# A zero fill by DMA: rows copied as they are, or rows cast from bf16 to f32

## The chip, the core and the metric

The kernel runs on one core of a Trainium2 chip. The metric is the device time of one execution in microseconds (us); the time before is the median of three runs, 823.16 us (822.59 to 823.45). One further view, a profile, records every instruction and every DMA transfer of one execution. In its pages PE is the matmul engine (PEld its weight loads), DVE the vector engine, ACT the scalar engine, POOL the engine that issues the zero fill, and SP the engine that issues most other DMAs. All DMAs, whoever issues them, are carried by the same 16 DMA engines.

## The reference

One decoder layer at decode time, forward and backward. Two sequences (B = 2) with one token each pass through layer norm, attention over a cached window, a residual, layer norm, a gated GELU network and a residual. Only the last 4,096 of 32,768 cached keys and values take part:

```python
W = min(4096, max(256, Sk // 4))              # Sk = 32768, so W = 4096
k = jnp.repeat(k_cache[:, :, Sk - W:, :], rep, axis=1)
v = jnp.repeat(v_cache[:, :, Sk - W:, :], rep, axis=1)
p = softmax(q @ k * Dh**-0.5);  o = p @ v
h = x + o @ wo;   h2 = h + B(layernorm(h))    # B: (gelu(x@wg) * (x@wu)) @ wd
```

The outputs are h2 and the gradients by the input, both caches and all weights. The gradient of each cache is as large as the cache (2 x 8 x 32768 x 128 in bf16, 134 MB), and its first 28,672 positions of every (sequence, head) are zero, because the window does not reach them. So the kernel must write 32 regions of 28,672 x 128 bf16 zeros, 7.34 MB each, 234.9 MB together.

## The kernel before

**The zero fill.** Line 99 makes a tile `zt` of 128 partitions x `ZE` bf16 elements, with `ZE` = 2048 (line 98), so 4 KiB in each partition. Line 122 fills it with zeros on DVE, by an AND with 0 of the first loaded weights (so it waits for the load of wq). Lines 186 and 187 call `zero_cast` once for each of the 32 regions; each call issues one DMA from POOL (line 104). The region is seen as 128 partitions x `nper` = 14 rows x 2048 elements, and the tile is repeated 14 times as the source, so a DMA consists of 1,792 rows of 4 KiB, and the whole fill of 57,344 rows. Source and destination are both bf16: nothing is converted. POOL issues the first eight DMAs in one go and each later one when an earlier one has landed.

**The rest of the work** runs beside the fill, in this order: layer norm and q; `attention(0)`, the loop over the eight key/value heads of sequence 0 (lines 309 to 446); `middle(0)`, output projection and feed-forward network forward and backward; `score_grads(0)`; then `attention(1)` and `middle(1)`; `score_grads(1)` with the weight gradients filled in; the gradients of wq (lines 717 to 754); and last the gradients of the caches' windows (lines 756 to 790), stored in 32 DMAs of 1 MB from SP (line 788). Keys, values and weights are loaded by SP (lines 116 to 145), each as soon as its place in SBUF is free.

**One large SBUF tile**, `mem`, holds nearly everything at hand-set offsets (lines 35 to 63); a place is reused when its last reader is done. The loop `m_unit` (lines 374 to 395) makes products of keys and exponentials in small buffers `pK` for the matmuls of line 394. It works on `pk_j` key columns at a time:

```python
for (n, h0, h1) in ((pk_j, 0, 2), (pk_j - 1, 2, 3)):
    ...  # DVE, line 380: two instructions a unit
for (jj, i) in [(jj, 3) for jj in range(pk_j)] + [(pk_j - 1, 2)]:
    ...  # ACT, line 383: pk_j + 1 instructions a unit
```

For sequence 0 `pk_j` is 4 and there are three buffers of 4 KiB; for sequence 1 it is 2, with three buffers of 2 KiB (lines 53 to 55). In both cases 32 columns of a head make up its `n_u` = 32 / `pk_j` units.

The end of the program waits, on SP, for all DMAs that write outputs, the zero fill's among them (it shows in the waits as line 813).

Of the kernel before, what the change touches and what calls it, by code (L numbers as in the profile page):

```python
# [8 lines left out]
F32 = mybir.dt.float32  # L9
# [7 lines left out]
P = 128  # L17
B, D = 2, 512
HQ, HKV, REP, DH = 32, 8, 4, 128
# [13 lines left out]
KIB = 1024  # L33

OFF_V = 0
OFF_M = 64 * KIB
# [3 lines left out]
OFF_WU = 150 * KIB  # L40
OFF_WD = 164 * KIB
OFF_R = 178 * KIB
OFF_KT = 186 * KIB
OFF_E = (190 * KIB, 192 * KIB)
OFF_DS = (194 * KIB, OFF_M)
MEM_BYTES = 196 * KIB
OFF_R0, OFF_R1, OFF_R2 = OFF_R, OFF_R + 2 * KIB, OFF_R + 4 * KIB
OFF_LN2B, OFF_XR = OFF_R + 6 * KIB, OFF_R + 7 * KIB
OFF_X, OFF_X_AGAIN = OFF_LN2B, OFF_M + 2 * KIB

K_OFF = ([OFF_WG + (g % 4) * 8 * KIB for g in range(HKV)],
         [OFF_WD, OFF_WD + 8 * KIB, 32 * KIB, 40 * KIB, 48 * KIB, 56 * KIB, OFF_WD, OFF_WD + 8 * KIB])
PK_J = (4, 2)
PK_OFF = ([OFF_WG + 32 * KIB + i * 4 * KIB for i in range(3)],
          [OFF_WD + 16 * KIB + i * 2 * KIB for i in range(3)])

OFF_BD = OFF_WO
OFF_GST = OFF_WG
# [7 lines left out]
def kernel(ctx, tc, A_x, A_k_cache, A_v_cache, A_wq, A_wo, B_x, B_w_gate, B_w_up, B_w_down, grad_out,  # L66
                out_0, out_1, out_2, out_3, out_4, out_5, out_6, out_7, out_8):
    nc = tc.nc
    Sk = A_k_cache.shape[2]
    Z = Sk - W  # L70
# [3 lines left out]
    mem_pool = ctx.enter_context(tc.tile_pool(name="mem", bufs=1))  # L74
    mem = mem_pool.tile([P, MEM_BYTES], U8)

    def at(off, shape, dt, name):
        n = int(np.prod(shape[1:])) * mybir.dt.size(dt)
        assert off + n <= MEM_BYTES, (name, off, n)
        ap = mem[0:shape[0], off:off + n].bitcast(dt)  # L80
        dims = " ".join(f"a{i}" for i in range(1, len(shape)))
        return ap.rearrange(f"p ({dims}) -> p {dims}", **{f"a{i}": shape[i] for i in range(1, len(shape))}) if len(shape) > 2 else ap
# [3 lines left out]
    def evac(out, in_):  # L86
        if evac_i[0] % 2 == 0:
            nc.vector.tensor_copy(out=out, in_=in_)  # L88
        else:
            nc.scalar.copy(out=out, in_=in_)  # L90
        evac_i[0] += 1
# [3 lines left out]
    dKv = out_2[:, :, Z:, :].rearrange("b g (p j) d -> p b g j d", p=P)  # L95
    dVv = out_3[:, :, Z:, :].rearrange("b g (p j) d -> p b g j d", p=P)

    ZE = 2048
    zt = const.tile([P, ZE], BF16)
    zero_regions = [o[b, g, 0:Z, :].rearrange("r d -> (r d)") for o in (out_2, out_3) for b in range(B) for g in range(HKV)]  # L100

    def zero_cast(i):
        nper = (Z * DH) // (P * ZE)
        nc.gpsimd.dma_start(out=zero_regions[i].rearrange("(p k e) -> p k e", p=P, k=nper),  # L104
                            in_=zt[:].unsqueeze(1).to_broadcast([P, nper, ZE]))

    dh2_x = at(OFF_XR, [66, D], BF16, "xr")
# [2 lines left out]
    def load_rows(eng):  # L110
        eng.dma_start(out=dh2_bf, in_=grad_out.rearrange("b s d -> (b s) d"))
        eng.dma_start(out=x_32, in_=A_x.rearrange("b s d -> (b s) d"))

    def load_x(off):
# [6 lines left out]
    load_rows(nc.scalar)  # L121
    nc.vector.tensor_scalar(out=zt[:].bitcast(U32), in0=wq_sb[:, 0, 0:ZE].bitcast(U32), scalar1=0, scalar2=None,
                            op0=ALU.bitwise_and)
# [62 lines left out]
    for i in range(len(zero_regions)):  # L186
        zero_cast(i)
# [40 lines left out]
    def tblock(ps_pool, src_block):  # L228
        ps = ps_pool.tile([P, 4, P], BF16, tag="ps_tb", name="ps_tb")
        for a in range(4):  # L230
            nc.tensor.transpose(out=ps[:, a, :], in_=src_block(a), identity=ident_bf[:])  # L231
        dst = at(OFF_KT + (tb_i[0] % 3) * KIB, [P, 4, P], BF16, "tb")
        tb_i[0] += 1
# [40 lines left out]
    M_sb = at(OFF_M, [P, HQ, DH], BF16, "M")  # L274
    E = [at(OFF_E[b], [P, 8, 4, HQ], BF16, f"e{b}") for b in range(B)]
    p_bf = [at(OFF_E[b], [P, 8 * P], BF16, f"p{b}") for b in range(B)]
    ds_bf = [at(OFF_DS[b], [P, 8 * P], BF16, f"ds{b}") for b in range(B)]

# [30 lines left out]
    def attention(b):  # L309
        with tc.tile_pool(name="ps_KT", bufs=2, space=PSUM) as ps_KT, \  # L310
# [16 lines left out]
            S_ps, Ef = {}, {}  # L327
            lsum = small.tile([P, 4, HQ], F32, name="lsum", tag="l4")
            eT = E[b]
            pk_j = PK_J[b]  # L330
            n_pk = len(PK_OFF[b])
            n_u = NJ // pk_j
            kt_every = n_u // 8
# [1 line left out]
            def kt_unit(g, u):  # L335
                KT_ps = ps_KT.tile([P, 8, P], BF16, tag="kt", name="KT_ps")
                for jj in range(8):
                    nc.tensor.transpose(out=KT_ps[:, jj, :], in_=Kt[b, g][:, u * 8 + jj, :], identity=ident_bf[:])  # L338
                KT = at(OFF_KT + (u % 2) * 2 * KIB, [P, 8, P], BF16, "KT")
                evac(KT[:], KT_ps[:])  # L340
# [119 lines left out]
    def middle(b):  # L460
        h0 = b * HQ
        with tc.tile_pool(name="ps_W", bufs=2, space=PSUM) as ps_W, \
# [80 lines left out]
            if b == 1:  # L543
                ffn_ps = ps_B.tile([B, D], F32)
                for k in range(NFR):
                    nc.tensor.matmul(out=ffn_ps[:], lhsT=actT_bf[:, k, :], rhs=wd[:, k, :], start=(k == 0), stop=(k == NFR - 1))
                h2_bf = at(OFF_KT + 3 * KIB, [B, D], BF16, "h2")
                nc.vector.tensor_tensor(out=h2_bf[:], in0=h_sb[:], in1=ffn_ps[:], op=ALU.add)
# [38 lines left out]
    def score_grads(b, filler=None):  # L587
# [4 lines left out]
        with tc.tile_pool(name="ps_S", bufs=1, space=PSUM) as ps_S, \  # L592
# [4 lines left out]
            def produce(i):  # L597
                g, a = units[i]
                VT_ps = ps_T.tile([P, 8, P], BF16, tag="t", name="VT_ps")
                for jj in range(8):  # L600
                    nc.tensor.transpose(out=VT_ps[:, jj, :], in_=Vt[b, g][:, a * 8 + jj, :], identity=ident_bf[:])  # L601
                VT = at(OFF_KT + (i % 2) * 2 * KIB, [P, 8, P], BF16, "VT")
                evac(VT[:], VT_ps[:])
# [18 lines left out]
    ln1_bf = at(OFF_R0, [B, D], BF16, "ln1b")  # L622
    mv1, rstd1 = layernorm(x_bf[:], "1", ln1, ln1_bf)
    attention(0)
    middle(0)
    score_grads(0)
    attention(1)
    middle(1)
    x_bf = load_x(OFF_X_AGAIN)
# [188 lines left out]
```

## Time and profile before

| | |
|---|---|
| median of three runs | 823.16 us (822.59 to 823.45) |
| the profiled execution | 823.45 us |
| its span in the profile | 821.7 us |
| PE / DVE / ACT / POOL busy | 596.9 / 513.5 / 457.4 / 36.3 us |
| moved by DMA | 332.50 MB, mean 405 GB/s |
| HBM read / written | 49.30 MB / 282.33 MB |
| the zero fill: DMAs, MB | 32 of 7.34 MB, issued from 14.5 to 574.3 us |
| last matmul phase ends, last store issued | about 750 us, 755.3 us |

The span is cut into 40 slices of about 20.5 us; in the rows with one digit for each slice, a 9 means 90% or more of the slice. The row DMA is the mean busy share of the 16 DMA engines. In the part on DMA queues, q0 (software) carries what POOL issues, which is the zero fill, and q1 (hardware) what SP issues; the three numbers are packets, megabytes, and the time of the packets as a share of 16 engines' span. A row of 4 KiB is one packet.

### The profile page before, as it was taken

How to read it: one execution, taken by the hardware profiler on the slowest of the kernel's cores; microseconds unless marked ns; L12 is line 12 of the kernel's file. 1: busy time of each engine (PE TensorE's matmuls, PEld its weight loads, DVE VectorE, ACT ScalarE, POOL GpSimd, SP SyncE). 2: the span in 40 equal slices, each digit the busy share in tenths (PEclk: the TensorE clock that was granted, in tenths of full speed). 3: DMA queues.
4: the chain of work that ended last, by engine and by line, in shares of the span. 5: the costliest groups of instructions: out<-in, count | busy, mean ns of one | idle time of the engine just before them, and what ended most of it. 6: DMA issues, size and time to landing. Idle time of an engine off the chain costs nothing.

```text
span 821.7 us, 13560 instructions
## 1 busy us (share of the span) xinstructions
PE 596.9 (73%) x5350; PEld 318.8 (39%) x5350; DVE 513.5 (62%) x1021; ACT 457.4 (56%) x1080; POOL 36.3 (4%) x51
## 2 busy tenths in 40 slices
PE   3788878789788588888857878988595777674000
PEld 3455443275766444444323457443241222221000
DVE  2799999433433499999961255667636899984000
ACT  1899999233334399999870333656443676674000
POOL 4100000000100000000000000000000000000000
PEclk9899999959579799999996775987586888897555
DMA  8999999999999999999999999999999999999995
GB/s 355 422 440 408 420 417 402 417 413 418 405 391 418 421 414 412 411 411 410 410 387 420 415 404 399 408 407 407 408 406 406 407 413 412 414 414 411 415 407 213
DMA packets 69472, 332.50 MB, mean 405 GB/s; under 512 B 1808, under 2 KB 1824, under 8 KB 59296
## 3 DMA queue, kind: packets, MB, share of 16 engines
q0 software_dynamic: 57856, 234.88, 71.3%
q1 hardware_dynamic: 11540, 96.75, 28.6%
q8 instruction: 42, 0.69, 0.3%
q14 instruction: 22, 0.18, 0.1%
q10 hardware_dynamic: 12, 0.01, 0.0%
HBM read 49.30 MB, written 282.33 MB: 404 GB/s over the span
## 4 chain that ended last, share of the span: by engine, by line
PE 41%; ACT 19%; DVE 17%; DMA 11%; issue 3%; SPq 0%; ACTq 0%; DVEq 0%
ACT mem L383 9%; ACT mem L90 9%; DVE mem L380 7%; PE ps_tb L231 7%; PE M_ps L394 6%; DMA out_dram<-mem 6%; DVE mem L88 4%; PE ps_g L780 3%; PE VT_ps L601 3%; PE dP_ps L610 3%; PE ps_gr L671 3%; PE KT_ps L338 2%; PE d_ln_ps L539 2%; PE gu_ps L487 2%; PE oPK_ps L388 2%
## 5 line engine op out<-in xcount | busy, mean ns | idle before, releaser
L380 DVE TENSOR_TENSOR mem<-mem,ef 128x128 bf16<-128x128 bf16 (+3 forms) x384 | 218.1, 615 | 9.3 <-PE M_ps L394 7.6
L383 ACT ACTIVATE mem<-mem,ef 128x128 bf16<-128x128 bf16 x704 | 214.6, 395 | 9.9 <-PE M_ps L394 9.3
L394 PE MATMUL M_ps<-mem 128*128 128x512 bf16 x512 | 155.9, 385 | 28.7 <-DVE mem L380 21.4
L780 PE MATMUL ps_g<-mem 128*128 128x512 bf16 x256 | 82.2, 424 | 26.7 <-ACT mem L90 25.5
L90 ACT COPY mem<-ps_tb 128x512 bf16<-128x512 bf16 x83 | 48.7, 586 | 94.4 <-PE ps_tb L231 72.4
L90 ACT CAST mem<-ps_g 128x512 bf16<-128x512 f32 x128 | 74.7, 586 | 34.5 <-DVE mem L88 30.2
L88 DVE CAST mem<-ps_g 128x512 bf16<-128x512 f32 x128 | 82.4, 687 | 11.9 <-PE ps_g L780 10.6
L231 PE MATMUL ps_tb<-ident_bf,mem 128*128 128x128 bf16 x664 | 80.5, 262 | 8.0 <-DVE mem L88 2.6
L88 DVE COPY mem<-ps_tb 128x512 bf16<-128x512 bf16 x83 | 35.2, 424 | 71.2 <-PE ps_tb L231 43.8
L394 PEld LDWEIGHTS <-mem 128*128 128x128 bf16 x512 | 43.9, 98 | 82.0 <-DVE mem L380 43.2
L231 PEld LDWEIGHTS <-mem 128*128 128x128 bf16 x664 | 54.6, 127 | 34.8 <-issue 26.5
L780 PEld LDWEIGHTS <-mem 128*128 128x128 bf16 x256 | 26.8, 105 | 81.3 <-issue 67.9
L104 POOL DMA_DIRECT2D out_dram<-zt x32 | 33.6, 1133 | 538.0 <-DMA out_dram<-zt 527.3
L338 PE MATMUL KT_ps<-ident_bf,mem 128*128 128x128 bf16 x512 | 49.6, 235 | 10.5 <-DMA mem<-in_A_k_cache_dram 4.6
L90 ACT COPY mem<-VT_ps 128x1024 bf16<-128x1024 bf16 x33 | 33.7, 1022 | 35.8 <-PE VT_ps L601 30.1
L610 PE MATMUL dP_ps<-mem 128*128 128x512 bf16 x128 | 43.1, 413 | 4.5 <-ACT mem L90 4.5
L601 PE MATMUL VT_ps<-ident_bf,mem 128*128 128x128 bf16 x512 | 44.4, 234 | 0.9 <-DVE pkT L577 0.9
L338 PEld LDWEIGHTS <-mem 128*128 128x128 bf16 x512 | 35.9, 105 | 23.6 <-issue 7.2
L601 PEld LDWEIGHTS <-mem 128*128 128x128 bf16 x512 | 36.1, 106 | 21.3 <-issue 13.3
L90 ACT COPY mem<-KT_ps 128x1024 bf16<-128x1024 bf16 x32 | 32.0, 1001 | 19.2 <-PE KT_ps L338 19.2
L671 PE MATMUL ps_gr<-mem 2*128 2x512 bf16 (+1 forms) x78 | 31.1, 471 | 13.4 <-DVE mem L691 7.2
L88 DVE COPY mem<-VT_ps 128x1024 bf16<-128x1024 bf16 x31 | 21.4, 690 | 29.1 <-PE VT_ps L601 28.5
(250 smaller groups left out, 646.6 us busy)
## 6 DMA issues: line engine op xcount, KB each, us to landing
out_dram<-zt POOLq DMA_DIRECT2D x32, 7168.0 KB, 174.6
out_dram<-mem SPq DMA_DIRECT2D x36, 1024.0 KB, 21.3
mem<-in_A_k_cache_dram SPq DMA_DIRECT2D x16, 1024.0 KB, 9.3
mem<-in_A_v_cache_dram SPq DMA_DIRECT2D x16, 1024.0 KB, 24.0
out_dram<-mem SPq DMA_DIRECT2D x5, 1792.0 KB, 10.9
mem<-in_A_wq_dram SPq DMA_DIRECT2D x1, 4096.0 KB
mem<-in_A_wo_dram SPq DMA_DIRECT2D x1, 4096.0 KB
mem<-in_B_w_down_dram SPq DMA_DIRECT2D x2, 1792.0 KB, 11.8
```

What stands on the lines that cost most here:

```text
L88: nc.vector.tensor_copy(out=out, in_=in_)
L90: nc.scalar.copy(out=out, in_=in_)
L104: nc.gpsimd.dma_start(out=zero_regions[i].rearrange("(p k e) -> p k e", p=P, k=nper), in_=zt[:].unsqueeze(1).to_broadcast([P, nper, ZE]))
L231: nc.tensor.transpose(out=ps[:, a, :], in_=src_block(a), identity=ident_bf[:])
L338: nc.tensor.transpose(out=KT_ps[:, jj, :], in_=Kt[b, g][:, u * 8 + jj, :], identity=ident_bf[:])
L380: nc.vector.tensor_tensor(out=pk[:, 0:n, h0:h1, :], in0=Kb[:, j0:j0 + n, :].unsqueeze(2).to_broadcast(shape), in1=ef[:, j0:j0 + n, h0:h1]. ...
L383: nc.scalar.activation(out=pk[:, jj, i, :], in_=Kb[:, j0 + jj, :], func=ACT.Copy, scale=ef[:, j0 + jj, i:i + 1])
L394: nc.tensor.matmul(out=M_ps[:], lhsT=Vt[b, g][:, j, :], rhs=pk[:, jj, :, :].rearrange("p i d -> p (i d)"), start=(j == 0), stop=(j == NJ - 1))
L601: nc.tensor.transpose(out=VT_ps[:, jj, :], in_=Vt[b, g][:, a * 8 + jj, :], identity=ident_bf[:])
L610: nc.tensor.matmul(out=dP_ps[:, c, :], lhsT=dOpad[:, w0:w0 + P], rhs=VT[:, c * 4:(c + 1) * 4, :].rearrange("d a k -> d (a k)"), start=(i = ...
L671: nc.tensor.matmul(out=ps[:, :n], lhsT=lhsT_fn(k), rhs=rhs_fn(k), start=True, stop=True)
L780: nc.tensor.matmul(out=ps[:, a2, :], lhsT=lhs_bf[:, jp * P:(jp + 1) * P], rhs=rhs_bd[:, ap * 2 + a2, gq * 4:(gq + 1) * 4, :].rearrange("q ...
```

## The change

The fill's tile becomes half as long (2 KiB in each partition), each region is seen as f32 instead of bf16 (two bf16 zeros are one f32 zero), and the DMA converts bf16 to f32 on the way. A row is now 2 KiB at the source and 4 KiB at the destination; there are still 14 rows for each partition and region. The 2 KiB for each partition that this frees go to `mem`, which grows by as much: the `pK` buffers of sequence 1 become two of 4 KiB instead of three of 2 KiB, `pk_j` is 4 for both sequences, and four offsets above them move up by 2 KiB.

```diff
-OFF_KT = 186 * KIB
-OFF_E = (190 * KIB, 192 * KIB)
-OFF_DS = (194 * KIB, OFF_M)
-MEM_BYTES = 196 * KIB
+OFF_KT = 188 * KIB
+OFF_E = (192 * KIB, 194 * KIB)
+OFF_DS = (196 * KIB, OFF_M)
+MEM_BYTES = 198 * KIB
...
-PK_J = (4, 2)
+PK_J = 4
 PK_OFF = ([OFF_WG + 32 * KIB + i * 4 * KIB for i in range(3)],
-          [OFF_WD + 16 * KIB + i * 2 * KIB for i in range(3)])
+          [OFF_WD + 16 * KIB + i * 4 * KIB for i in range(2)])
...
-    ZE = 2048
+    ZE = 1024
     zt = const.tile([P, ZE], BF16)
...
     def zero_cast(i):
-        nper = (Z * DH) // (P * ZE)
-        nc.gpsimd.dma_start(out=zero_regions[i].rearrange("(p k e) -> p k e", p=P, k=nper),
+        nper = (Z * DH // 2) // (P * ZE)
+        nc.gpsimd.dma_start(out=zero_regions[i].bitcast(F32).rearrange("(p k e) -> p k e", p=P, k=nper),
                             in_=zt[:].unsqueeze(1).to_broadcast([P, nper, ZE]))
...
-            pk_j = PK_J[b]
+            pk_j = PK_J
```

## The prediction

> **What bounds the kernel now.** I read the page's slices and its part on DMA queues first, because a fill of 235 MB is a matter of DMA.
>
> ```profile
> PE   3788878789788588888857878988595777674000
> DMA  8999999999999999999999999999999999999995
> GB/s 355 422 440 408 420 417 402 417 413 418 405 391 418 421 414 412 411 411 410 410 387 420 415 404 399 408 407 407 408 406 406 407 413 412 414 414 411 415 407 213
> ...
> q0 software_dynamic: 57856, 234.88, 71.3%
> q1 hardware_dynamic: 11540, 96.75, 28.6%
> ```
>
> The DMA engines are full from the second slice to the last but one, while PE has nothing to do in the last three. The shares of q0 and q1 sum to 99.9% of the span: all 16 engines move packets, one after the other, for as long as the kernel runs. The end is set by that sum, not by the chain of compute. The windows of the last 120 us show it from the other side (columns: length; busy time and count of PE, weight loads, DVE, ACT, POOL; clock; DMA share; GB/s).
>
> ```profile
> 740.00:750.00 10.00, 8.18 (x25) 2.61 (x23) 8.43 (x13) 7.89 (x14) 0.00 (x0) 0.83 1.01 410
> 750.00:760.00 10.00, 0.00 (x0) 0.00 (x0) 0.00 (x0) 0.20 (x1) 0.00 (x0) 0.69 1.02 415
> ...
> 795.00:800.00 5.00, 0.00 (x0) 0.00 (x0) 0.00 (x0) 0.00 (x0) 0.00 (x0) 0.50 1.01 405
> 800.00:805.00 5.00, 0.00 (x0) 0.00 (x0) 0.00 (x0) 0.00 (x0) 0.00 (x0) 0.50 0.99 400
> 805.00:810.00 5.00, 0.00 (x0) 0.00 (x0) 0.00 (x0) 0.00 (x0) 0.00 (x0) 0.50 0.74 302
> 810.00:815.00 5.00, 0.00 (x0) 0.00 (x0) 0.00 (x0) 0.00 (x0) 0.00 (x0) 0.50 0.49 203
> ```
>
> The engines have stopped computing at 750 us; the last store (line 788) is issued at 755.3 us and those stores take at most 31.2 us to land, so they are done by about 786.5 us. What runs after that is zero fill. The waits name it:
>
> ```profile
> SPq L813 <- DMA out_dram<-zt: 64.2, 1, 64.2
> ```
>
> SP's last wait, 64.2 us long, is for the fill; POOL's row in the waits has 24 waits for landed fills, 527.3 us, so the fill always had more DMAs queued than the engines could take. So a nanosecond more or less for a fill row moves the end, and compute has about 35 us of cover (821.7 - 786.5).
>
> **What a row costs.** The two queue rows give two averages. q0: 0.713 x 821.7 us x 16 engines / 57,856 packets = 162.0 ns for 4,060 bytes. q1: 0.286 x 821.7 x 16 / 11,540 = 325.8 ns for 8,384 bytes. A straight line through both is 8.2 ns a packet plus 0.0379 ns a byte (26.4 bytes a ns). A 4 KiB row costs 8.2 + 155.2 = 163.4 ns, and 57,344 of them / 16 engines give 585.6 us. One nanosecond on each row is 57,344 / 16 = 3.58 us of the kernel. This rate is the same for q1, which holds loads and stores, as for the fill, and in the stretch where loads and fill alternate it hardly rises:
>
> ```profile
> 40.00:60.00 20.00, 17.10 (x207) 9.92 (x211) 19.61 (x33) 19.86 (x61) 0.00 (x0) 1.00 1.03 431
> ```
>
> A load writes SBUF and the fill reads it. Had each direction a lane of its own, the stretch would run far above the 401 GB/s that the line gives for rows of 4 KiB alone (4,096 bytes x 16 / 163.4 ns). So I take the limit to lie inside a DMA engine, which takes one packet after the other. What the rows before cannot show is which side of the packet its clock counts, because every packet before has equal bytes on both sides.
>
> **The change, part by part.**
>
> *The cast.* No transfer before converts, so its price is bounded from both sides. If the source bytes set the time, a row costs 8.2 + 77.6 = 85.8 ns, 77.6 ns less, 278 us off the DMA sum. If reading 2 KiB and writing 4 KiB follow each other, it costs 77.6 ns more, 278 us on the sum. Between these ends the nearest row is the 4 KiB copy: the same bytes written to the same places, by the same queue and in the same number of packets. I take its written 4,096 bytes as what sets the time, and for the conversion something between nothing and one more fixed cost of a packet (8.2 ns; that is also what a row would cost if it were cut in two). Because the copy is the nearest row, I stay near the lower end and take a quarter, 2 ns: 2 x 3.58 = +7.2 us.
>
> One rule of the Trainium skill speaks for much more. The row first: 404 GB/s over the span, of which 235 MB leave SBUF as fill. The page "DMA: Bandwidth & Descriptors", section "Where 436 GB/s comes from", puts the limit at the 16 SBUF ports, 435.2 GB/s together. By it, the 117.4 MB that the fill would still read from SBUF take an estimated 270 us, and DMA would stop being the bound. By the row of the mixed stretch (431 GB/s in both directions together) it is not the port but the engine that is full, and the sum above stands.
>
> *The smaller tile.* Line 122 (694 ns on DVE for 1,024 words) halves: -0.35 us before the first fill issue at 14.5 us. The DMA engines are then busy with K and V loads (399 GB/s from 14 to 24 us), which hide it. Nothing.
>
> *Issue.* 32 DMAs as before, of 1,792 rows each. POOL is busy for 36.3 us in all, 1.04 us for nearly all issues, with eight DMAs in flight; an issue that took several times as long would still be ahead of the engines. Nothing; without that cover it would be its whole extra time once for each of 24 issues.
>
> *`pk_j` 2 to 4 in `attention(1)`.* For four columns DVE ran two instructions of 512 (686 ns each) and two of 128 (284 ns), 1,940 ns; now one of 1,024 (1,208 ns) and one of 384 (542 ns), 1,750 ns. ACT ran six of 395 ns, 2.37 us; now five, 1.98 us. In the chain a head takes about 18.2 us in `attention(1)` (the pieces at 320.23, 338.47 and 356.72 us) and 15.8 us in `attention(0)` (49.64, 65.38 and 81.16 us), which has the same form with three buffers: 8 x 2.4 = 19 us at most. Two buffers instead of three: a buffer's round is its products (1.98 us) plus four matmuls of line 394 (4 x 0.385 = 1.54 us), 3.5 us, and two of them in turn give a unit each 1.76 us, under ACT's 1.98, so they need not become the bound. If filling and use did not overlap at all, 8 units x 3.5 = 28 us a head, 78 us more in all; that would pass the 35 us of cover by 43 us. On the path that sets the end neither counts as long as the fill ends last: nothing. No queue is reordered; SP's loads and stores come in the same order, and the moved offsets do not change which buffers overlap in time in a way that adds a wait on that path.
>
> **Sum.** Span 821.7 + 7.2 = 828.9 us. The profiled execution's own time is 1.75 us above its span, 823.45, and 0.29 us above the median of 823.16; against the median the sum is **830.3 us**. The forecast's own range is 823 (conversion free) to 853 us (a full 8.2 ns, 29.4 us).
>
> **The rivals.**
>
> *A, not slower: the short read hides the fixed cost.* If the 8.2 ns of a packet lie on its reading side, and the read of 2 KiB is over in half the time, the gap between packets vanishes behind the write. For it speaks that the line has such a constant at all; against it that nothing tells on which side it lies. Price: -8.2 x 3.58 = -29.4 us, **794 us**. It decides from the point where the reading side, with its fixed cost, is shorter than the write (85.8 against 155.2 ns), which it would be. Compute's end at 786.5 us still comes before.
>
> *B, much faster: source bytes set the time.* The fill is 278 us less, the DMA sum 543 us, and the chain takes over. Its end at 786.5 us falls by the waits for DMA in it: 44.3 us (11.80 for wd, 11.29 for K, 9.37 for x, 11.85 for a store), where a load's share beside the fill rises from 318.5 / (318.5 + 163.4) = 66% to 79%, so by 7 us; and 68.3 us (9.74, 27.35 and the last landing of 31.2) after the fill is over, by a third, 23 us. `pk_j` then counts, 19 us. **737 us**, with 700 to 775 as its range. Against it speaks the mixed stretch.
>
> *C, much slower: converting is a pass of its own.* The engine handles elements more slowly than bytes, or writes only when the read is complete. It decides from 8.2 ns a row on; its far end is 77.6 ns, 823 + 278 = **1,101 us**. Against it: nothing in the trace before, which has no such transfer.
>
> *That the change does not do what it says* would be rows cut into more packets; cut in two, it is the forecast's upper end, 853 us.
>
> **How the numbers follow.** Forecast 0.50 (of it 0.18 with so little added, under 0.46 ns a row, that the time stays within 0.2%, which is about what a measurement of this kernel can tell from no change, and 0.32 slower), A 0.24, B 0.12, C 0.14. Faster 0.36, same 0.18, slower 0.46. The range takes in the forecast and A, the top of B (0.04) and the near part of C (0.05): 770 to 890 us, 0.83. Since signs are mixed, the likeliest case's own range is 823 to 853.
>
> **What would show it.** The queue rows after: q0's share times the span, over the packets, gives the time of a row; forecast 165.4 ns, A 155, B 86, C over 172. The packet count of q0 shows whether rows are cut. If `attention(1)` has heads of about 15.8 us, the `pk_j` step is right; if SP's last wait is still for the fill, the cover held. Wrong would be the whole approach if the last slices show idle DMA engines or if SP's last wait is for a store: then the chain, not the fill, sets the end.

## The result, and the profile after

The changed kernel takes 831.4 us (median of four runs, 830.67 to 833.47) against 822.88 us in runs of the kernel before on the same chip: a ratio of 1.0107, with a 95% interval of 1.0088 to 1.0127. The forecast was 830.3 us. The number is right, but the profile shows another path to it than the one forecast.

The slices and queue rows of the changed kernel's page, the counterpart of those shown for the kernel before:

```profile
span 830.0 us, 13381 instructions
PE   3788767818888826886777347889787793777682
DMA  8999999999999999999999999999999999476968
GB/s 362 415 429 408 422 423 423 424 424 422 423 422 421 415 422 422 421 423 421 423 421 424 423 426 423 424 421 423 423 423 424 427 422 408 166 290 278 398 267 349
q0 software_dynamic: 57856, 234.88, 82.3%
q1 hardware_dynamic: 11540, 96.75, 51.3%
```

Until slice 33 the DMA engines move 421 to 426 GB/s in most slices, where they moved mostly 400 to 420 before. From about 715 us on the fill moves no more than one engine's share (26 GB/s from 715 to 720 us); its last row ends at 727.0 us. In the last six slices the DMA engines are partly idle, but for one slice, while PE is busy until about 816 us. The shares of q0 and q1 now sum to 134% of the span: the records of packets overlap, so a share is no longer a cost. The windows of 50 to 700 us, before and then after, show the rate (last column, GB/s) and the overlap (DMA share):

```profile
50.00:700.00 650.00, 526.89 (x4717) 283.89 (x4716) 439.22 (x893) 392.77 (x942) 24.94 (x24) 0.85 1.02 410
```

```profile
50.00:700.00 650.00, 473.14 (x4570) 273.90 (x4569) 377.35 (x679) 336.61 (x809) 25.04 (x24) 0.81 1.49 422
```

For the fill alone I took all stretches of 2 us between 20 and 700 us in which SP moved no data: 410.8 GB/s before, 423.0 after. A row of 4 KiB then costs 4,096 x 16 / 410.8 = 159.5 ns before and 154.9 ns after: the fill became cheaper by 4.6 ns a row. The end, though, is no longer the fill's. SP's last wait in the changed kernel:

```profile
SPq L813 <- DMA out_dram<-mem: 8.6, 4, 2.4
```

It is for a store, not for `zt`. And the chain that sets the end now has long pieces of waiting for DMA (start, length in us, what landed), among them a load of x that is 2 KB in size. The first fence is the same load of x in the kernel before, the second the changed kernel:

```profile
423.96 9.37 DMA mem<-in_A_x_dram
```

```profile
383.14 27.43 DMA mem<-in_A_v_cache_dram
426.40 23.82 DMA mem<-in_A_v_cache_dram
464.77 22.16 DMA mem<-in_A_x_dram
577.83 18.02 DMA out_dram<-mem
688.24 18.35 DMA out_dram<-mem
```

SP's timeline shows how this adds up. The load of wd for sequence 0 and the next load, which waits for work that needs wd, before and after (start, length, what):

```profile
151.03 0.33 SPq L141 DMA_DIRECT2D mem<-in_B_w_down_dram  x1
177.23 0.33 SPq L129 DMA_DIRECT2D mem<-in_A_k_cache_dram  x1
```

```profile
158.32 0.33 SPq L141 DMA_DIRECT2D mem<-in_B_w_down_dram  x1
198.50 0.33 SPq L129 DMA_DIRECT2D mem<-in_A_k_cache_dram  x1
```

The lateness grows from 7.3 us to 21.3 us over one landing; wd took 25.4 us to land instead of 11.8. By the reload of x for the last stages (line 116) it is 54.7 us (560.63 against 505.97), at the first cache-gradient store 69.7 us (723.40 against 653.67), and the last of these stores is issued at 818.2 us instead of 755.3: 62.9 us late. It lands within 10.3 us, since the fill is over, where these stores took up to 31.2 us before; SP's last data end at 828.2 us instead of 786.2, and that is the end.

**What holds the landings.** In the trace's DMA records each DMA of SP ends with packets of 4 bytes, one for each engine it used: its completion. Before, such a record of q1 was 8.9 ns long in the mean and 25 ns at most. After, the mean is 2,277 ns and the longest 17.1 us; 352 of them exceed 0.3 us, and 264 of these end within 20 ns of the end of a 4-byte record of q0, which is the completion of a fill DMA on some engine. A fill DMA has 1,792 / 16 = 112 rows on each engine, 112 x 154.9 ns = 17.4 us. The load of wd shows it directly. Its data are through 11.4 us after the issue (11.2 before), at 169.7 us; its 16 completion packets start between 168.3 and 169.8 us, but end between 179.5 and 183.3, each 11 to 15 us long (9 ns before). So the theory to test was this. **H**: the data of a load or store pass between the fill's rows, but its completion on an engine is held until the fill DMA that runs there has completed, up to 17.4 us. The rivals were **S**: the converting row takes more of an engine (192 ns in its record against 159, medians), so that other transfers get less of it; and **L**: the two `pK` buffers made compute late.

### The profile page after: what moved, and what is told of

Same layout as the page of the kernel before. It is cut to its first block, busy times and chain, and to the rows that moved or that the text cites. A ratio compares the mean times of both kernels' runs of the same rounds, so it can differ in the third digit from the quotient of the medians.

```text
span 830.0 us, 13381 instructions
## 1 busy us (share of the span) xinstructions
PE 589.6 (71%) x5350; PEld 324.1 (39%) x5350; DVE 508.9 (61%) x893; ACT 442.3 (53%) x1016; POOL 36.5 (4%) x51
## 3 DMA queue, kind: packets, MB, share of 16 engines
q0 software_dynamic: 57856, 234.88, 82.3%
## 4 chain that ended last, share of the span: by engine, by line
PE 25%; DVE 14%; DMA 13%; ACT 5%; issue 2%; ACTq 0%; DVEq 0%; SPq 0%
DMA mem<-in_A_v_cache_dram 6%; ACT mem L90 5%; DVE mem L88 4%; DMA out_dram<-mem 4%; PE ps_g L780 4%; DVE mem L380 4%; PE ps_tb L231 4%; DMA mem<-in_A_x_dram 3%; PE ps_gr L671 2%; PE M_ps L394 2%; PE VT_ps L601 2%; DVE mem L259 2%; PE dP_ps L610 2%; PE d_ln_ps L728 1%; PE attn_ps L473 1%
## 5 line engine op out<-in xcount | busy, mean ns | idle before, releaser
L380 DVE TENSOR_TENSOR mem<-mem,ef 128x1024 bf16<-128x1024 bf16 (+1 forms) x256 | 213.4, 874 | 14.5 <-PE M_ps L394 14.3
L383 ACT ACTIVATE mem<-mem,ef 128x128 bf16<-128x128 bf16 x640 | 199.5, 391 | 18.6 <-PE M_ps L394 16.5
L394 PE MATMUL M_ps<-mem 128*128 128x512 bf16 x512 | 139.0, 391 | 33.6 <-DVE mem L380 31.7
L231 PE MATMUL ps_tb<-ident_bf,mem 128*128 128x128 bf16 x664 | 81.7, 266 | 23.6 <-DMA mem<-in_B_w_down_dram 16.5
L338 PE MATMUL KT_ps<-ident_bf,mem 128*128 128x128 bf16 x512 | 47.3, 246 | 33.2 <-DMA mem<-in_A_k_cache_dram 24.3
L671 PE MATMUL ps_gr<-mem 2*128 2x512 bf16 (+1 forms) x78 | 31.2, 473 | 18.3 <-DVE mem L88 7.8
L88 DVE CAST mem<-ps_gr 128x512 bf16<-128x512 f32 (+1 forms) x40 | 26.5, 669 | 24.0 <-PE ps_gr L671 16.9
## 6 DMA issues: line engine op xcount, KB each, us to landing
mem<-in_B_w_down_dram SPq DMA_DIRECT2D x2, 1792.0 KB, 25.4
```

The lines of the kernel that those rows point to most:

```text
L380: nc.vector.tensor_tensor(out=pk[:, 0:n, h0:h1, :], in0=Kb[:, j0:j0 + n, :].unsqueeze(2).to_broadcast(shape), in1=ef[:, j0:j0 + n, h0:h1]. ...
L383: nc.scalar.activation(out=pk[:, jj, i, :], in_=Kb[:, j0 + jj, :], func=ACT.Copy, scale=ef[:, j0 + jj, i:i + 1])
L394: nc.tensor.matmul(out=M_ps[:], lhsT=Vt[b, g][:, j, :], rhs=pk[:, jj, :, :].rearrange("p i d -> p (i d)"), start=(j == 0), stop=(j == NJ - 1))
L671: nc.tensor.matmul(out=ps[:, :n], lhsT=lhsT_fn(k), rhs=rhs_fn(k), start=True, stop=True)
```

## The experiments

**Conversion alone.** The kernel before with the fill of the change; `pk_j`, its buffers and offsets as before.

```diff
-    ZE = 2048
+    ZE = 1024
...
-        nper = (Z * DH) // (P * ZE)
-        nc.gpsimd.dma_start(out=zero_regions[i].rearrange("(p k e) -> p k e", p=P, k=nper),
+        nper = (Z * DH // 2) // (P * ZE)
+        nc.gpsimd.dma_start(out=zero_regions[i].bitcast(F32).rearrange("(p k e) -> p k e", p=P, k=nper),
```

> The kernel before with the conversion alone: fill tile of 2 KiB, bf16 to f32, but pk_j and its buffers as before. Theory H: a store's or load's completion on a DMA engine is held until the fill DMA that runs on that engine has completed, and the chain of compute, late by such holds, sets the end. Then the holds stay, the heads of attention(1) take 18.2 us again where they do not wait for V, and the time is 831 to 850 us, with q1's 4-byte packets as long as in the changed kernel (mean 2.3 us). Rival L: the two pK buffers made compute late; then it is faster than the changed kernel, about 795 us (row of 155 ns, fill last).

Measured: 870.95 us, ratio 1.0574 (1.0558 to 1.059). L falls: without the new buffers the kernel is slower than the changed one by 39.5 us, not faster. The completions are held nearly as in the changed kernel (1.89 us in the mean, 16.8 us at most). The direction is H's, the size is more than the expected 831 to 850 us. The chain (the same columns as above) has the first K and four waits for V of sequence 1 on it:

```profile
290.84 25.50 DMA mem<-in_A_k_cache_dram
372.96 23.69 DMA mem<-in_A_v_cache_dram
403.16 25.03 DMA mem<-in_A_v_cache_dram
434.38 25.39 DMA mem<-in_A_v_cache_dram
465.64 27.20 DMA mem<-in_A_v_cache_dram
```

The first K is not what sets the two kernels apart: in both, PE waits 18 to 19 us for it, and the first head of sequence 1 starts at 316.4 us. By the load of x at the end of `attention(1)` this kernel is 51.2 us behind (515.99 against 464.77 us). PE's waits for V (total, times, longest, in us), in the changed kernel and then here, account for 33.6 us of it; the rest is near the 19 us that the prediction gave for eight longer heads.

```profile
PE oPK_ps L388 <- DMA mem<-in_A_v_cache_dram: 14.6, 4, 5.5
```

```profile
PE oPK_ps L388 <- DMA mem<-in_A_v_cache_dram: 48.2, 4, 13.8
```

**Seven pieces, converting.** The changed kernel, with the fill of a region issued as seven DMAs.

```diff
-        nc.gpsimd.dma_start(out=zero_regions[i].bitcast(F32).rearrange("(p k e) -> p k e", p=P, k=nper),
-                            in_=zt[:].unsqueeze(1).to_broadcast([P, nper, ZE]))
+        dst = zero_regions[i].bitcast(F32).rearrange("(p k e) -> p k e", p=P, k=nper)
+        step = nper // 7
+        for k0 in range(0, nper, step):
+            nc.gpsimd.dma_start(out=dst[:, k0:k0 + step, :],
+                                in_=zt[:].unsqueeze(1).to_broadcast([P, step, ZE]))
```

> The changed kernel with each region's fill cut into 7 DMAs of 2 rows per partition (224 DMAs of 1.05 MB instead of 32 of 7.34 MB). Theory H: a hold lasts at most a seventh of the 17 us that a fill DMA stays on its engines, 2.5 us; the chain is then about 19 us earlier than before the change, and the end goes back to the fill with rows of 155 ns: 785 to 805 us. Rival S: SP's transfers are slow because a converting row takes more of an engine (192 ns in the records against 163); then cutting the DMAs changes nothing: 831 us, or a little more for the added issues.

Measured: 815.67 us, ratio to the kernel before 0.9903 (0.9888 to 0.9918). The rows' records are as long as in the changed kernel (191 ns against 192, medians) and still overlap, but the chain is back before the fill and the fill ends last again, as SP's last wait shows (this kernel's line 816 is the same wait):

```profile
SPq L816 <- DMA out_dram<-zt: 69.0, 1, 69.0
```

S falls: nothing was done to the rows, only to the number of DMAs that they come in. The time is above the expected 785 to 805 us; the next run (the cut itself has a price) and the end of the cut in two (one engine works on alone) say why.

**Seven pieces, copying.** The same cut in the kernel before.

```diff
-        nc.gpsimd.dma_start(out=zero_regions[i].rearrange("(p k e) -> p k e", p=P, k=nper),
-                            in_=zt[:].unsqueeze(1).to_broadcast([P, nper, ZE]))
+        dst = zero_regions[i].rearrange("(p k e) -> p k e", p=P, k=nper)
+        step = nper // 7
+        for k0 in range(0, nper, step):
+            nc.gpsimd.dma_start(out=dst[:, k0:k0 + step, :],
+                                in_=zt[:].unsqueeze(1).to_broadcast([P, step, ZE]))
```

> The kernel before with the same cut into 7 DMAs for each region, no conversion. A control: H expects no holds to shorten (q1's 4-byte packets took 8.9 ns before), so 823 us within 3; a clear gain here would mean that the cut itself, not the holds, is what helps.

Measured: 831.39 us, ratio 1.0093 (1.0077 to 1.011). So the cut by itself costs 7.7 us where there are no holds to shorten, against the expectation of none; its 4-byte records of q1 are 8.9 ns as before. POOL still waits for landings with eight DMAs in flight, which now are 8.4 MB of work instead of 58.7 MB; but from 50 to 700 us the engines are as full as before (share 1.02 in both, 407 GB/s against 410), and from 780 to 805 us their share is 0.96 to 1.01 where it was 0.99 to 1.02, so they hardly run dry. What makes the rows a little slower stays open. The two kernels in seven pieces both end with the fill, and the converting one is 15.7 us faster: 4.4 ns for each row, close to the 4.6 ns above.

**A conversion that keeps the sizes.** The kernel before, with the destination seen as fp16.

```diff
-        nc.gpsimd.dma_start(out=zero_regions[i].rearrange("(p k e) -> p k e", p=P, k=nper),
+        nc.gpsimd.dma_start(out=zero_regions[i].bitcast(mybir.dt.float16).rearrange("(p k e) -> p k e", p=P, k=nper),
```

> The kernel before with a conversion that changes no sizes: the fill's destination is seen as fp16, so bf16 is converted to fp16, rows of 4 KiB on both sides. If the holds come from conversion as such, q1's 4-byte packets are long and the chain is late, 840 to 870 us, since the rows are no shorter at the source. If the holds come from short reads that run ahead of their writes, there are none and the time is 823 us. The row itself: 163 ns if the gain to 155 came from the shorter read, 155 ns if it came from the converting path.

Measured: 825.2 us, ratio 1.0019 (1.001 to 1.0028). Queue rows and the rate per slice:

```profile
GB/s 356 415 421 415 420 422 408 405 414 419 403 389 416 419 415 411 410 413 410 410 395 411 416 402 400 411 404 406 408 406 405 407 413 411 413 413 411 415 408 227
q0 software_dynamic: 57856, 234.88, 77.6%
q1 hardware_dynamic: 11540, 96.75, 29.3%
```

The rate is that of the copy, not 423 GB/s (411.8 in stretches without data of SP), and the 4-byte records of q1 are 22 ns in the mean. So conversion as such neither speeds the row nor holds completions for long; both come with a source that is shorter than what is written. (All kernels with such a source write f32; a fill from f32 to f32 was not tried.) The records overlap more than the copy's (share 1.09 from 50 to 700 us, against 1.02).

**Two and four pieces, converting.** As for seven, with `step = nper // 2`; and with bounds 0, 4, 8, 11, 14.

> The changed kernel with each region's fill cut in two (64 DMAs of 3.67 MB). Theory H: a hold lasts up to 8.7 us instead of 17.4; q1's 4-byte packets have a mean between those of 32 DMAs (2.28 us) and of 224 (0.47 us), about 1.2 us. The chain is late by about half of what it was, its last store still lands near 790 us, and the fill with rows of 155 ns ends about there too; the cut costs less than the 7.7 us that seven pieces cost the copying kernel, about 1 to 2. So 795 to 810 us, faster than seven pieces. Rival S (no holds, only slower rows): 831 us.

> The changed kernel with four pieces for each region (rows 4, 4, 3, 3 of each partition; 128 DMAs). Theory H: holds up to 5 us, 4-byte packets of q1 about 0.7 us in the mean; the fill sets the end, the cut costs about half of seven pieces' 7.7 us: 797 to 810 us, between two pieces and seven.

Measured: two pieces 812.81 us, ratio 0.9867 (0.9852 to 0.9882), the fastest kernel of the study; four pieces 814.13 us, 0.9886 (0.9869 to 0.9902). The completion records follow the size of the fill DMA. The third column is the rows that the largest fill DMA has on one engine, times 154.9 ns:

| fill DMAs | kernel | rows of one DMA on an engine | q1's 4-byte records: mean | longest | time |
|---|---|---|---|---|---|
| 32 | changed | 112 = 17.4 us | 2.28 us | 17.1 us | 831.4 us |
| 64 | two pieces | 56 = 8.7 us | 1.14 us | 8.6 us | 812.8 us |
| 128 | four pieces | 32 = 5.0 us | 0.71 us | 4.8 us | 814.1 us |
| 224 | seven pieces | 16 = 2.5 us | 0.47 us | 2.3 us | 815.7 us |
| 32 | conversion alone | 112 = 17.4 us | 1.89 us | 16.8 us | 870.95 us |
| 32 | u8 source (below) | 112 = 17.4 us | 1.95 us | 17.6 us | 854.45 us |
| 64 | conversion alone, two pieces (below) | 56 = 8.7 us | 1.10 us | 8.8 us | 821.2 us |
| 32 | same-width conversion | 112 | 0.022 us | 0.35 us | 825.2 us |
| 224 | copying | 16 | 0.009 us | 0.025 us | 831.4 us |

The longest hold is, in all seven kernels with a short source, within 0.6 us of the time that one fill DMA stays on an engine. This is as close as these runs come to the mechanism; what inside the engine waits, they do not show. The changed kernel in two, four and seven pieces ends with the fill each time, two pieces with 812.8 us where 795 to 810 were expected; the windows of its end show what is missing:

```profile
795.00:800.00 5.00, 0.00 (x0) 0.00 (x0) 0.00 (x0) 0.00 (x0) 0.00 (x0) 0.50 0.07 26
800.00:805.00 5.00, 0.00 (x0) 0.00 (x0) 0.00 (x0) 0.00 (x0) 0.00 (x0) 0.50 0.07 27
805.00:811.00 6.00, 0.00 (x0) 0.00 (x0) 0.00 (x0) 0.00 (x0) 0.00 (x0) 0.50 0.08 17
```

A share of 0.07 is one engine of 16, and 26 GB/s is a sixteenth of 420: by this rate, fifteen engines are done at about 795 us, inside the expected range, and one works alone for some 15 us more (a record does not name its engine). The expectation had spread the fill's rows evenly to the last. The kernel before ends less abruptly: its rate falls in steps from 805 us on (302 GB/s, then 203).

**One byte at the source.** The changed kernel with `zt` in u8: rows of 1 KiB, converted to f32, 32 DMAs.

```diff
-    zt = const.tile([P, ZE], BF16)
+    zt = const.tile([P, ZE], U8)
...
-    nc.vector.tensor_scalar(out=zt[:].bitcast(U32), in0=wq_sb[:, 0, 0:ZE].bitcast(U32), scalar1=0, scalar2=None,
+    nc.vector.tensor_scalar(out=zt[:].bitcast(U32), in0=wq_sb[:, 0, 0:ZE // 2].bitcast(U32), scalar1=0, scalar2=None,
```

> The changed kernel with a source of one byte per element: rows of 1 KiB in SBUF, converted from u8 to f32, still 32 DMAs. If the written 4 KiB set the row, its cost stays at 155 ns and the DMA rate at about 423 GB/s, the holds stay, and the time is 825 to 845 us. If what is read sets part of it, the rate rises above 430 GB/s and the fill is over earlier than at 715 us.

Measured: 854.45 us, ratio 1.0374 (1.0359 to 1.039). The rate:

```profile
GB/s 368 415 425 413 424 421 423 425 423 424 421 422 422 415 422 422 421 423 421 423 424 423 424 424 423 424 423 422 424 422 430 419 354 106 109 261 330 357 280 349
```

Until the fill runs out it is again 421 to 425 GB/s in most slices: with half as much to read as in the change, the row costs the same. So, as far as these runs go, the written 4 KiB set the row once the read is shorter. The time lies above the expected range: two waits for V on its chain are 29.6 and 31.9 us. Why these are longer than in the changed kernel, while the longest hold is the same (17.6 us), stays open.

**Conversion alone, two pieces.** The kernel of the first experiment with the cut in two.

```diff
...
+        dst = zero_regions[i].bitcast(F32).rearrange("(p k e) -> p k e", p=P, k=nper)
+        step = nper // 2
...
```

> Conversion alone (pk_j and buffers as before the change) with each region cut in two. It gives the worth of the pk_j step when the holds are halved: in the changed kernel as it is, the conversion alone cost 39.5 us more (870.95 against 831.4). If pk_j counts only where the chain sets the end, the difference to the same cut with pk_j 4 shrinks to under 15 us: 800 to 820 us.

Measured: 821.23 us, ratio 0.9969 (0.9933 to 1.0004), just above the expected range. This is the median of ten runs that scatter from 815.7 to 826.9 us, far more than those of any other kernel here; why is not known. In the profiled one (824.8 us) SP's last wait is for a store:

```profile
SPq L816 <- DMA out_dram<-mem: 7.7, 4, 2.4
```

So in this one the chain sets the end, and `pk_j` 4 brings it in front of the fill: that is worth 8.4 us by the medians (821.23 - 812.81), 3 to 14 us by the scatter, against 39.5 us with whole regions. What the step is worth where the fill ends last with either `pk_j`, as the prediction had it, no run shows. With the copying fill it was not tried: the longer tile and the larger buffers together need 2 KiB more in each partition than either kernel holds.

## Why the prediction was right, and where it was not

**The bound before** was read rightly: the fill ends last, and the sum of the packets sets its end. That held for the kernel before, for the copying fill in seven pieces, for the same-width conversion, and for the changed kernel in two, four and seven pieces.

**The row** was mis-sized, and with the wrong sign. The forecast added 2 ns to it; it fell by 4.6 ns (159.5 to 154.9), 57,344 x 4.6 / 16 = 16.5 us off the fill, and the two kernels in seven pieces differ by as much, 15.7 us. Rival A had the sign and the level (155 ns) right, but its -29.4 us is nearly twice what was gained. The reason is the base: 163.4 ns is the mean length of a record, and the records before are not strictly one after the other; the share of 1.02 in the windows says that they overlap by about 2%, so that a row's true cost was nearer 160 ns. The u8 run fits A's ground, a write that sets the row, and the same-width run shows that the shorter read is needed for it; that the part gained is the fixed cost of a packet is not shown. B, source bytes setting the time, is excluded by the u8 run; C, as a cost of converting, by the changed kernel's own rate.

**The cover** is the step that failed. The prediction gave compute 35 us of cover and treated the chain as untouched by the cast, because "No queue is reordered". It counted what a fill row costs the engines and not what it costs the transfers beside it. The held completions made the chain 62.9 us late at its last store, and 42.0 us at the landing (828.2 against 786.2 us); that used up the cover and passed the fill, which itself had become shorter. The two errors, a row forecast 10.5 ns too dear (165.4 against 154.9) and a chain without its holds, end by coincidence 1 us from the measured time. What the prediction named as proof against itself did happen: the last slices show idle DMA engines, and SP's last wait is for a store. The test that it announced by q0's share, on the other hand, would have misled: 0.823 x 830.0 x 16 / 57,856 = 189 ns would have spoken for C, while the rate says 155: with overlapping records the share is no price.

**`pk_j`** was right in its mechanism: the heads of `attention(1)` that do not wait for V are 15.8 us apart (the chain's pieces at 342.21, 357.98 and 373.75 us), as forecast with two buffers. Its worth was put at nothing, for the cover; with the cover gone it was not 19 us but 39.5, since with the longer heads PE also waits 48.2 us for V instead of 14.6. **The smaller tile** (427 ns instead of 694) and **the issue** (1.04 us as before) cost nothing, as said.

**The rule weighed.** The 423 GB/s with the u8 source, where the fill reads a quarter of what it writes, decide against the sum by the SBUF ports that the prediction weighed: by that sum less reading would have left the DMA engines idle in part, and they stay at the same rate. The Trainium skill's page "DMA: Bandwidth & Descriptors", section "Queues, rings and completion order", says that the write of a completion is strongly ordered and lands only after every earlier write of that DMA engine, in whatever queue. If so, it would account for a completion that waits behind fill rows whose reads have run ahead of their writes; the runs agree in so far as holds appear only where the read is shorter than the write, but they do not show reads running ahead. That a hold ends with the fill DMA, at 17.1, 8.6, 4.8 and 2.3 us, is the runs' own finding.

## What to carry to other kernels

A background transfer has two prices: the engine time of its rows and the delay that it puts on the completions of other transfers; ask for the second one before writing that nothing else changes. Where a DMA expands its source, keep each one short (here two pieces of 3.67 MB for a region): it gave 812.8 us instead of 831.4. And a right number is no proof of its steps; look at what ends last before believing it.

## What the runs showed of the hardware that was not expected

- A 4 KiB row written by an expanding DMA costs 154.9 ns instead of 159.5 (423 GB/s against 411, in stretches without data of SP), with 2 KiB and with 1 KiB read; a same-width conversion does not gain it (412 GB/s).
- The completions of SP's DMAs waited up to 17.1 us beside such a fill, and up to 8.6, 4.8 and 2.3 us with shorter fill DMAs; a 2 KB load took 22 us on the chain.
- Cutting a copying fill into seven times as many DMAs, eight in flight, cost 7.7 us; why stays open.
- By the rate, one DMA engine of the 16 finishes some 15 us after the others (26 GB/s from 795 to 811 us in the kernel with two pieces).
